# Joint image and text attention: x tile 3 loaded and transposed later, the last value chunk by key tile, one narrow value unit moved ahead of the shift strip

## The chip, the cores and the metric

The kernel runs on one core of one Trainium2 chip. The metric is device time in microseconds (us); the time before is the median of three runs, 116.81 us (116.59 to 117.2). The engines are named as in the profile: PE (TensorE, matrix products; PEld is its loading of the stationary operand), DVE (VectorE), ACT (ScalarE), POOL (GpSimd) and SP (SyncE, which here only issues loads and stores). Each engine takes its instructions in the order in which the program gives them to it, and waits for other engines through semaphores.

## The reference

Inputs are bf16: two batches of 256 image tokens and 32 text tokens, width D = 1152, a condition vector `c` for each batch, and for image and text each a modulation weight (D x 6D, of which the first three column blocks matter: shift, scale, gate), a query-key-value weight (D x 3D) and an output weight (D x D).

```python
mod = silu(c) @ wmod                       # shift, scale, gate
h   = layernorm(x) * (1 + scale) + shift   # image and text each
q, k, v = split(h @ wqkv)                  # image and text each
# tokens of text and image joined, one head of width D
p   = softmax(q @ k.T * D ** -0.5)
a   = p @ v
out = x + gate * (a @ wo)                  # image and text each
```

The change concerns the part up to the image values `v`.

## The kernel before

The 512 image tokens are four x tiles of 128 tokens (tiles 0 and 1 are batch 0, tiles 2 and 3 batch 1). The width D is nine key tiles of 128 rows (`KT`). The image values need the normalised x, transposed (so that width lies on the partitions) and multiplied by 1 + scale; the shift is left out of `hT_i` at first and comes in later, so that the value products can begin before the shift weights are there. The value product of a token tile is cut into three units of columns: two wide ones of 512 columns, written (tile, 0) and (tile, 1), and a narrow one of 128 columns (`v_rest`, line 339).

The weights come in four chunks of key tiles, `KC = [(0, 2), (2, 4), (4, 6), (6, 9)]`: of the scale weights the columns of these key tiles (`load_sc`), of the value weights their rows (`load_v`). All these loads stand in one queue, SP's, in the order of lines 103 to 114: x tiles 0 and 1, scale chunk 0, x tile 2, value chunk 0, x tile 3, then scale and value chunks in turn; the last value chunk comes in two pieces, key tile 6 and key tiles 7 and 8. Behind them come the shift weights (`w_sh_i`), the query weights and the rest.

The order of work is written out by hand (`manual_schedule`); there is no planner. For each x tile, DVE computes statistics in three pieces (`stats_of`, line 162), ACT takes the root (`std_of`, line 169), and DVE writes the normalised tile (`out_of`, lines 173 and 174). PE transposes it in nine steps (`x_transposes`, line 187): for tiles 1 to 3 the first eight go to one buffer of the pool `ps_mm` and the ninth to the single buffer of `ps_sm`. ACT empties them into `hT_i`: `evac_scaled` (line 192) multiplies by 1 + scale while it copies, one instruction for each key tile, `evac_low` (line 196) copies the other key tiles of the first buffer unscaled, in one instruction, and `evac_high` (line 199) the ninth. `mod_scale` (line 207) computes the scale factors of one chunk on PE and adds 1 on DVE (line 213); `apply_mod` (lines 223 to 232) then multiplies what was copied unscaled, on DVE, POOL or ACT by its last argument.

`v_part` (line 238) adds one chunk's key tiles to a wide unit. A unit holds its `ps_mm` buffer from its first chunk until its copy into `v_i` after the last (line 247; `evac`, lines 153 and 155, takes DVE and ACT in turn). `ps_mm` has seven buffers. Seven wide units are accumulated side by side (`SEVEN`): those of tiles 0 to 2, and (3, 0), which begins when tile 3's transposes have been copied out of theirs. The eighth, (3, 1), follows by itself (line 394).

Behind it comes the shift strip: `rows_for_cols` multiplies the shift weights as rows with the 32 columns of the condition (lines 367 and 371) and copies them on DVE; `select_cols` (lines 383 and 385) turns these rows into columns on PE, and `cols_out` writes them on DVE. Between strip and selection PE computes the narrow units of tiles 2 and 3, behind the selection those of tiles 0 and 1; then the shift is added to `hT_i` by three engines (lines 223, 226, 230), and the query products follow (line 444).

Of the kernel before, what the change touches and what calls it, by code (L numbers as in the profile page):

```python
# [14 lines left out]
def kernel(  # L15
# [14 lines left out]
    nc = tc.nc  # L30
# [4 lines left out]
    B, NI, D = x_img.shape  # L35
    NT = x_txt.shape[1]
    P = 128
    KT = D // P
    NTOK = NI + NT
    NIT = (B * NI) // P  # L40
    TPB = NI // P
    NTT = B * NT
    CH = 384
    NCH = D // CH
# [4 lines left out]
    KC = [(0, 2), (2, 4), (4, 6), (6, KT)]  # L49
    VW = 512  # L50
    NM = 1024
# [18 lines left out]
    def w_view(src):  # L70
        return src.rearrange("(kt p) n -> p kt n", p=P)
# [20 lines left out]
    def load_x(i):  # L92
        nc.sync.dma_start(x_i[:, i, :], xi_t[:, i, :])

    def load_sc(ch):
        k0, k1 = KC[ch]
        nc.sync.dma_start(w_sc_i[:, :, k0 * P:k1 * P], w_view(wmod_img)[:, :, D + k0 * P:D + k1 * P])

    def load_v(ch):
        k0, k1 = KC[ch]  # L100
        nc.sync.dma_start(w_v_i[:, k0:k1, :], w_view(wqkv_img)[:, k0:k1, 2 * D:3 * D])
# [3 lines left out]
    load_sc(0)  # L105
    load_x(2)
    load_v(0)
    load_x(3)
    for ch in range(1, len(KC)):
        load_sc(ch)  # L110
        if ch < len(KC) - 1:
            load_v(ch)
    for k0, k1 in ((6, 7), (7, KT)):
        nc.sync.dma_start(w_v_i[:, k0:k1, :], w_view(wqkv_img)[:, k0:k1, 2 * D:3 * D])
    K3 = ((0, 3), (3, 6), (6, KT))
# [35 lines left out]
    def evac(out_ap, in_ap):  # L151
        if evac_idx[0] % 2 == 0:
            nc.vector.tensor_copy(out_ap, in_ap)  # L153
        else:
            nc.scalar.copy(out_ap, in_ap)  # L155
        evac_idx[0] += 1

    def ln_stats(x_ap, np_, k0=0, k1=NCH, stats=None):
        if stats is None:
            stats = small.tile([P, NCH, 6], f32, tag="stats")  # L160
        for k in range(k0, k1):
            nc.vector.bn_stats(stats[0:np_, k, :], x_ap[:, k * CH:(k + 1) * CH])  # L162
        return stats

    def ln_std(stats, np_):
        mv = small.tile([P, 2], f32, tag="mv")
        nc.vector.bn_aggr(mv[0:np_, :], stats[0:np_, :, :])
        rstd = small.tile([P, 1], f32, tag="rstd")
        nc.scalar.activation(rstd[0:np_, :], mv[0:np_, 1:2], ACT.Sqrt, bias=eps_t[0:np_, :])
        return mv, rstd  # L170
# [10 lines left out]
    def x_transposes(i, n0=5):  # L181
        tps = (ps_mm.tile([P, n0, P], bf, tag="mm", name="tp"),
               ps_mm.tile([P, KT - n0, P], bf, tag="mm", name="tp") if n0 == 5 else
               ps_sm.tile([P, KT - n0, P], bf, tag="sm", name="tp"))
        for kt in range(KT):
            tp = tps[0][:, kt, :] if kt < n0 else tps[1][:, kt - n0, :]
            nc.tensor.transpose(tp, xn_i[:, i, kt * P:(kt + 1) * P], ident[:])  # L187
        return tps + (n0,)

    def evac_scaled(i, tps, n):  # L190
        for kt in range(n):
            nc.scalar.activation(hT_i[:, kt, i * P:(i + 1) * P], tps[0][:, kt, :], ACT.Identity,  # L192
                                 scale=mod_i[:, KT + kt, i // TPB:i // TPB + 1])

    def evac_low(i, tps, n):
        nc.scalar.copy(hT_i[:, n:tps[2], i * P:(i + 1) * P], tps[0][:, n:tps[2], :])

    def evac_high(i, tps):
        nc.scalar.copy(hT_i[:, tps[2]:KT, i * P:(i + 1) * P], tps[1][:])

    def mod_cols(wt, out_ps, j0, j1):
        for j in range(j0, j1):
            for kt in range(KT):
                nc.tensor.matmul(out_ps[:, j - j0, :], lhsT=wt[:, kt, j * P:(j + 1) * P], rhs=sT[:, kt, :],  # L204
                                 start=(kt == 0), stop=(kt == KT - 1))

    def mod_scale(ch, eng, own=True):
        k0, k1 = KC[ch]
        pool, tag = (ps_sm, "sm") if own else (ps_mm, "mm")
        mps = pool.tile([P, KT, B], f32, tag=tag)  # L210
        mod_cols(w_sc_i, mps, k0, k1)
        if eng == "dve":
            nc.vector.tensor_scalar_add(mod_i[:, KT + k0:KT + k1, :], mps[:, 0:k1 - k0, :], 1.0)  # L213
        else:
            nc.scalar.activation(mod_i[:, KT + k0:KT + k1, :], mps[:, 0:k1 - k0, :], ACT.Identity, bias=1.0)

    def apply_mod(kt, t0, t1, shift, eng):
        b = t0 // TPB
        sl = hT_i[:, kt, t0 * P:t1 * P]
        ap = mod_i[:, kt, b:b + 1] if shift else mod_i[:, KT + kt, b:b + 1]  # L220
        op = ALU.add if shift else ALU.mult
        if eng == 0:
            nc.vector.tensor_scalar(sl, sl, ap, None, op0=op)
        elif eng == 1:
            if shift:
                nc.gpsimd.tensor_scalar(sl, sl, 1.0, ap, op0=ALU.mult, op1=ALU.add)
            else:
                nc.gpsimd.tensor_scalar(sl, sl, ap, 0.0, op0=ALU.mult, op1=ALU.add)  # L228
        elif shift:
            nc.scalar.activation(sl, sl, ACT.Identity, bias=ap, scale=1.0)  # L230
        else:
            nc.scalar.activation(sl, sl, ACT.Identity, scale=ap)
# [2 lines left out]

    vacc = {}

    def v_part(i, half, ch):
        k0, k1 = KC[ch]
        if ch == 0:  # L240
            vacc[i, half] = ps_mm.tile([P, VW], f32, tag="mm", name=f"va{i}{half}")
        ps = vacc[i, half]
        for kt in range(k0, k1):
            nc.tensor.matmul(ps[:], lhsT=hT_i[:, kt, i * P:(i + 1) * P], rhs=w_v_i[:, kt, half * VW:(half + 1) * VW],  # L244
                             start=(kt == 0), stop=(kt == KT - 1))
        if k1 == KT:
            evac(v_i[:, i, half * VW:(half + 1) * VW], ps[:])


    def v_block(units, chs):  # L250
        for ch in chs:
            for (i, half) in units:
                v_part(i, half, ch)
# [6 lines left out]
    def stats_of(i, k0, k1):  # L260
        lns[i] = ln_stats(x_i[:, i, :], P, k0, k1, lns.get(i))

    def std_of(i):
        lns[i] = ln_std(lns[i], P)

    def out_of(i):
        ln_apply(x_i[:, i, :], P, xn_i[:, i, :], *lns[i])
# [19 lines left out]
    v_block([(0, 0), (0, 1), (1, 0), (1, 1)], [0])  # L287
    evac_low(1, tp1, 2)
    tps = x_transposes(2, KT - 1)
    stats_of(3, 0, NCH)  # L290
    evac_scaled(2, tps, 2)
    std_of(3)
    mod_scale(1, "dve", own=False)
    for n, kt in enumerate(range(*KC[1])):
        apply_mod(kt, 0, 2, False, n)
    evac_low(2, tps, 2)
    evac_high(2, tps)
    v_block([(2, 0), (2, 1)], [0])
    out_of(3)
    for kt in range(*KC[1]):  # L300
        apply_mod(kt, 2, 3, False, 0)
    v_block([(0, 0), (0, 1)], [1])
    tps = x_transposes(3, KT - 1)
    evac_high(3, tps)
    evac_scaled(3, tps, 4)
    evac_low(3, tps, 4)
    v_block([(1, 0), (1, 1)], [1])
    mod_scale(2, "dve")
    for kt in range(*KC[2]):
        apply_mod(kt, 0, 2, False, 0)  # L310
        apply_mod(kt, 2, 4, False, 1)
    v_block([(2, 0), (2, 1)], [1])
    v_block([(3, 0)], [0, 1])
    v_i = act.tile([P, NIT, D], bf, tag="A")
    SEVEN = [(i, half) for i in range(NIT) for half in range(2)][:7]
    for (i, half) in SEVEN[:5]:
        v_part(i, half, 2)
    mod_scale(3, "dve")
    for b in range(B):
        for n, kt in enumerate(range(*KC[3])):  # L320
            apply_mod(kt, b * TPB, (b + 1) * TPB, False, (n + b) % 3)
    for (i, half) in SEVEN[5:]:
        v_part(i, half, 2)
    for (i, half) in SEVEN:
        v_part(i, half, 3)

    for b in range(B):
        nc.gpsimd.tensor_copy(sTw[:, :, b, :], sT[:, :, b:b + 1].to_broadcast([P, KT, NT // 2]))  # L330
# [8 lines left out]
    def v_rest(i0, i1):  # L339
        ps = ps_mm.tile([P, TPB, P], f32, tag="mm")  # L340
        for kt in range(KT):
            for i in range(i0, i1):
                nc.tensor.matmul(ps[:, i - i0, :], lhsT=hT_i[:, kt, i * P:(i + 1) * P], rhs=w_v_i[:, kt, NM:D],  # L343
                                 start=(kt == 0 and i == i0), stop=(kt == KT - 1 and i == i1 - 1))
        return ps

    def v_rest_out(i0, i1, ps):
        evac(v_i[:, i0:i1, NM:D], ps[:])

    NGG = 4  # L350
    RC = 2 * P
# [23 lines left out]
    def rows_for_cols(wt, nm, lhs=None):  # L375
        gps = strip_rows(wt, sT32 if lhs is None else lhs)
        g_sb = work.tile([P, RC + P], bf, tag=nm, bufs=1, name=nm)
        evac(g_sb[:], gps[:])
        return g_sb
# [12 lines left out]
    ps = ps_mm.tile([P, VW], f32, tag="mm")  # L392
    for kt in range(KT):
        nc.tensor.matmul(ps[:], lhsT=hT_i[:, kt, 3 * P:4 * P], rhs=w_v_i[:, kt, VW:NM], start=(kt == 0), stop=(kt == KT - 1))  # L394
    evac(v_i[:, 3, VW:NM], ps[:])
    shr = rows_for_cols(w_sh_i, "shr")
    cps = ps_sm.tile([P, NCOL + B], f32, tag="sm")
    v_rest_out(TPB, NIT, v_rest(TPB, NIT))
    select_cols(shr, cps)
    cols_out(mod_i[:, 0:KT, :], cps, 0.0)  # L400
    vr = v_rest(0, TPB)
# [94 lines left out]
    for blk, wq in enumerate([w_q_t, w_k_t]):  # L496
        for j0 in range(0, KT, FG):
            jn = min(FG, KT - j0)
            ps = ps_mm.tile([P, FG, NTT], f32, tag="mm")
# [342 lines left out]
```

## Time and profile before

| | us |
|---|---|
| median of three runs | 116.81 (116.59 to 117.2) |
| the profiled execution | 116.89 |
| its span | 114.9 |
| PE busy | 108.6 (95%) |
| DVE, ACT, POOL busy | 53.4, 34.5, 28.0 |
| granted TensorE clock | 1.0 throughout |
| first matmul with a scale chunk | 8.03 |
| first wide value matmul | 10.23 |
| scale chunk 3's matmuls | 20.65 |
| shift strip | 28.76 |
| first query matmul | 32.11 |

The profile is of one execution. Its times count from the start of the span, and the measured time has some 2 us around the span. A line of the order of time has start, length, engine, line of the kernel, operation, the tiles written and read, and the count of instructions merged into it; in brackets stands how long the engine was idle before it and what ended that. Matmuls are pipelined: each wide one is given as 0.379 us though the next starts 0.216 us later, so the pace is read from start to start. A few records of matmuls are missing.

### The profile page before, as it was taken

To read this page: it belongs to the slowest core of one execution; us is meant where nothing else is said; L and a number is where in the kernel's file an instruction comes from. 1 tells how busy PE (TensorE), PEld (TensorE's weight loads), DVE (VectorE), ACT (ScalarE), POOL (GpSimd) and SP (SyncE) were. 2 spreads that over 40 slices of the span, in tenths; PEclk is the share of its full clock that TensorE was granted. 3 is DMA by queue.
4 is the path that set the end of the run, shared out by engine and by line. 5 is a ranking of instruction groups with operands and counts; after the bars stand their busy time and mean duration, and the time that the engine had idled before them with its cause. 6 is when DMAs were issued, how large, how long until landed. Compare 5 with 4: busy or idle time off the path is not lost.

```text
span 114.9 us, 2934 instructions
## 1 busy us (share of the span) xinstructions
PE 108.6 (95%) x1248; PEld 65.4 (57%) x1255; DVE 53.4 (47%) x137; ACT 34.5 (30%) x84; POOL 28.0 (24%) x59
## 2 busy tenths in 40 slices
PE   5948999999999999999999999999999999999990
PEld 1325564544954444477444545987788656667670
DVE  1687921354290212211742242136675813998571
ACT  2818960342380320121270221115565710001000
POOL 7000103460060000001315000000460460999100
DMA  3999999999999999999999999999999999962142
GB/s 87 276 362 361 371 384 377 411 412 411 411 404 405 412 416 402 412 412 411 405 408 412 396 411 410 406 410 405 411 408 407 407 411 397 388 244 106 37 157 69
DMA packets 22744, 40.89 MB, mean 356 GB/s; under 512 B 1279, under 2 KB 6539, under 8 KB 22731
## 3 DMA queue, kind: packets, MB, share of 16 engines
q1 hardware_dynamic: 21648, 39.64, 90.4%
q0 software_dynamic: 608, 0.88, 2.1%
q10 hardware_dynamic: 475, 0.18, 0.6%
q8 instruction: 10, 0.16, 0.5%
q14 instruction: 3, 0.02, 0.1%
HBM read 39.36 MB, written 1.34 MB: 354 GB/s over the span
## 4 chain that ended last, share of the span: by engine, by line
PE 90%; DMA 6%; SPq 1%; issue 1%; ACT 0%; DVE 0%
PE qkps L444 30%; PE ps L764 15%; PE va L244 12%; DMA w_sc_i<-in_wmod_img_dram 6%; PE aps L672 5%; PE ps L502 4%; PE sps L528 4%; PE gps L367 4%; PE mps L204 2%; PE ops L782 2%; PE ps L343 2%; PE tp L187 2%; PE ps L603 2%; PE ps L394 2%; PE gps L737 1%; PE sps L541 1%
## 5 line engine op out<-in xcount | busy, mean ns | idle before, releaser
L444 PE MATMUL qkps<-hT_i,t 128*128 128x512 bf16 x158 | 35.4, 379 | 0.2
L444 PEld LDWEIGHTS <-t 128*128 128x128 bf16 x162 | 15.6, 98 | 18.3
L764 PE MATMUL ps<-t,aT 128*128 128x384 bf16 x99 | 16.4, 326 | 0.0
L764 PEld LDWEIGHTS <-aT 128*128 128x128 bf16 x117 | 11.0, 98 | 6.9 <-issue 0.5
L244 PE MATMUL va<-w_v_i,hT_i 128*128 128x512 bf16 x60 | 14.1, 379 | 0.5 <-ACT hT_i L192 0.4
L748 POOL TENSOR_TENSOR w_og<-t,gb 128x384 bf16<-128x384 bf16 x9 | 8.8, 1016 | 4.1 <-issue 4.1
L244 PEld LDWEIGHTS <-hT_i 128*128 128x128 bf16 x63 | 5.8, 97 | 7.0 <-POOL hT_i L228 0.5
L770 DVE TENSOR_TENSOR tmp<-ps,gb 128x384 bf16<-128x384 f32 x11 | 6.1, 550 | 6.1 <-DMA gb<-mod_scratch 4.4
L428 DVE TENSOR_SCALAR qkT<-qkps 128x512 bf16<-128x512 f32 x4 | 2.8, 692 | 11.6 <-PE qkps L444 11.6
L162 DVE BATCH_NORM_STATS2 stats<-x_i 128x6 f32<-128x384 bf16 x12 | 5.8, 544 | 2.9 <-DMA x_i<-in_x_img_dram 2.9
L430 ACT ACTIVATE qkT<-qkps 128x512 bf16<-128x512 f32 x5 | 2.9, 596 | 13.5 <-PE qkps L444 13.5
L139 PE MATMUL wps<-wz 128*128 128x512 bf16 x16 | 5.6, 497 | 1.2 <-DVE wz L127 1.2
L228 POOL TENSOR_SCALAR hT_i<-hT_i,mod_img 128x256 bf16<-128x256 bf16 x5 | 2.5, 513 | 16.2 <-DVE mod_img L213 12.8
L153 DVE CAST qkT<-qkps 128x512 bf16<-128x512 f32 x4 | 2.8, 692 | 7.7 <-PE qkps L444 7.7
L155 ACT CAST qkT<-qkps 128x512 bf16<-128x512 f32 x5 | 2.8, 588 | 10.6 <-PE qkps L444 10.6
L522 POOL COPY px<-pb 128x64 bf16<-128x64 bf16 x4 | 1.0, 238 | 19.8 <-DVE pb L520 19.8
L771 DVE TENSOR_TENSOR o<-tmp,x_i 128x384 bf16<-128x384 bf16 x11 | 5.4, 486 | 0.4
L455 POOL TENSOR_SCALAR svn<-svr 128x128 bf16<-128x128 bf16 x1 | 0.3, 300 | 20.6 <-DVE svr L153 20.6
L685 DVE TENSOR_SCALAR aT<-aps,sv 128x288 bf16<-128x288 f32 (+2 forms) x11 | 4.3, 457 | 2.0 <-PE aps L672 2.0
L502 PEld LDWEIGHTS <-t 128*128 128x128 bf16 x162 | 4.9, 98 | 0.2
L502 PE MATMUL ps<-hT_t,t 128*128 128x64 bf16 x162 | 4.9, 193 | 0.0
L672 PE MATMUL aps<-pT,v_i 128*128 128x288 bf16 (+2 forms) x44 | 4.8, 264 | 0.0
(159 smaller groups left out, 143.7 us busy)
## 6 DMA issues: line engine op xcount, KB each, us to landing
t<-in_wmod_txt_dram SPq DMA_DIRECT2D x3, 2592.0 KB, 22.0
t<-in_wmod_img_dram SPq DMA_DIRECT2D x2, 2592.0 KB, 23.3
t<-in_wqkv_img_dram SPq DMA_DIRECT2D x6, 864.0 KB, 14.1
t<-in_wqkv_txt_dram SPq DMA_DIRECT2D x2, 2592.0 KB, 17.2
t<-in_wqkv_txt_dram SPq DMA_DIRECT2D x3, 864.0 KB, 14.5
t<-in_wo_img_dram SPq DMA_DIRECT2D x1, 2592.0 KB
t<-in_wo_txt_dram SPq DMA_DIRECT2D x3, 864.0 KB, 15.4
w_v_i<-in_wqkv_img_dram SPq DMA_DIRECT2D x4, 576.0 KB, 7.8
```

What stands on the lines that cost most here:

```text
L139: nc.tensor.matmul(ps[:], lhsT=wz[:, 0:P], rhs=wz[:], start=True, stop=True)
L162: nc.vector.bn_stats(stats[0:np_, k, :], x_ap[:, k * CH:(k + 1) * CH])
L244: nc.tensor.matmul(ps[:], lhsT=hT_i[:, kt, i * P:(i + 1) * P], rhs=w_v_i[:, kt, half * VW:(half + 1) * VW], start=(kt == 0), stop=(kt == K ...
L367: nc.tensor.matmul(gps[32 * g:32 * g + 32, 0:RC], lhsT=lhs[:, kt, :], rhs=wt[:, kt, g * RC:(g + 1) * RC], start=(kt == 0), stop=(kt == KT ...
L444: nc.tensor.matmul(pss[j - j0][:], lhsT=wq[:, kt, j * P:(j + 1) * P], rhs=hT_i[:, kt, :], start=(kt == 0), stop=(kt == KT - 1))
L502: nc.tensor.matmul(ps[:, j - j0, :], lhsT=wq[:, kt, j * P:(j + 1) * P], rhs=hT_t[:, kt, :], start=(kt == 0), stop=(kt == KT - 1))
L528: nc.tensor.matmul(sps[:], lhsT=qkT[:, ft, b, q0:q0 + P], rhs=qkT[:, KT + ft, b, :], start=(ft == 0), stop=(ft == KT - 1))
L672: nc.tensor.matmul(bank[:, off:off + c1 - c0], lhsT=lhsT, rhs=rhs, start=(first[id(bank)] == n), stop=(final[id(bank)] == n))
L748: nc.gpsimd.tensor_mul(w_og[:, dt, 0:CH], w_o_i[:, dt, NG0:D], gb[:, B - 1, NG0:D])
L764: nc.tensor.matmul(ps[:, 0:cw], lhsT=aT[:, dt, t0:t0 + P], rhs=rhs, start=(dt == DTS[0]), stop=(dt == DTS[-1]))
L770: nc.vector.tensor_mul(tmp[:, 0:cw], ps[:, 0:cw], gb[:, b, cs])
L771: nc.vector.tensor_add(o[:, cs], tmp[:, 0:cw], x_i[:, i, cs])
```

## The change

Four things are moved; the set of matmuls and loads stays the same.

- x tile 3 is loaded behind value chunk 1 instead of behind value chunk 0.
- Its statistics, root and normalisation move on DVE and ACT behind the multiplications of chunk 1; its transposes move on PE behind all chunk-1 matmuls and the scale factors of chunk 2. Six of its key tiles, not four, are now scaled while they are copied, so chunk 2's later multiplications cover only tiles 0 to 2. The matmuls of (3, 0) for chunks 0 and 1 move behind the five units' chunk 2.
- The last chunk runs over its key tiles in two passes, key tile 6 for all seven units, then key tiles 7 and 8; before, each unit took its three key tiles at once.
- The narrow unit of tile 2 moves ahead of the shift strip, with a copy of its own on DVE; only that of tile 3 stays between strip and selection.

```diff
     load_v(0)
-    load_x(3)
     for ch in range(1, len(KC)):
         load_sc(ch)
         if ch < len(KC) - 1:
             load_v(ch)
+        if ch == 1:
+            load_x(3)
...
-    def v_part(i, half, ch):
-        k0, k1 = KC[ch]
+    def v_part(i, half, ch, kts=None):
+        k0, k1 = kts or KC[ch]
...
     tps = x_transposes(2, KT - 1)
-    stats_of(3, 0, NCH)
     evac_scaled(2, tps, 2)
-    std_of(3)
     mod_scale(1, "dve", own=False)
     for n, kt in enumerate(range(*KC[1])):
         apply_mod(kt, 0, 2, False, n)
     evac_low(2, tps, 2)
     evac_high(2, tps)
     v_block([(2, 0), (2, 1)], [0])
-    out_of(3)
     for kt in range(*KC[1]):
         apply_mod(kt, 2, 3, False, 0)
-    v_block([(0, 0), (0, 1)], [1])
-    tps = x_transposes(3, KT - 1)
-    evac_high(3, tps)
-    evac_scaled(3, tps, 4)
-    evac_low(3, tps, 4)
-    v_block([(1, 0), (1, 1)], [1])
+    stats_of(3, 0, NCH)
+    std_of(3)
+    out_of(3)
+    v_block([(0, 0), (0, 1), (1, 0), (1, 1), (2, 0), (2, 1)], [1])
     mod_scale(2, "dve")
     for kt in range(*KC[2]):
         apply_mod(kt, 0, 2, False, 0)
-        apply_mod(kt, 2, 4, False, 1)
-    v_block([(2, 0), (2, 1)], [1])
-    v_block([(3, 0)], [0, 1])
+        apply_mod(kt, 2, 3, False, 1)
+    tps = x_transposes(3, KT - 1)
+    evac_high(3, tps)
+    evac_scaled(3, tps, 6)
+    evac_low(3, tps, 6)
     v_i = act.tile([P, NIT, D], bf, tag="A")
     SEVEN = [(i, half) for i in range(NIT) for half in range(2)][:7]
     for (i, half) in SEVEN[:5]:
         v_part(i, half, 2)
+    v_block([(3, 0)], [0, 1])
     mod_scale(3, "dve")
...
     for (i, half) in SEVEN[5:]:
         v_part(i, half, 2)
-    for (i, half) in SEVEN:
-        v_part(i, half, 3)
+    k0, k1 = KC[3]
+    for kts in ((k0, k0 + 1), (k0 + 1, k1)):
+        for (i, half) in SEVEN:
+            v_part(i, half, 3, kts)
...
     def v_rest_out(i0, i1, ps):
-        evac(v_i[:, i0:i1, NM:D], ps[:])
+        evac(v_i[:, i0:i1, NM:D], ps[:, 0:i1 - i0, :])
...
     evac(v_i[:, 3, VW:NM], ps[:])
+    vr = v_rest(TPB, TPB + 1)
+    nc.vector.tensor_copy(v_i[:, TPB:TPB + 1, NM:D], vr[:, 0:1, :])
     shr = rows_for_cols(w_sh_i, "shr")
     cps = ps_sm.tile([P, NCOL + B], f32, tag="sm")
-    v_rest_out(TPB, NIT, v_rest(TPB, NIT))
+    v_rest_out(TPB + 1, NIT, v_rest(TPB + 1, NIT))
     select_cols(shr, cps)
```

## The prediction

> **What bounds the kernel now.** I read the chain that ended last first, because it says which engine a gain must come from; then the order of time between 10 and 33 us, which is where the change lies; then the landing times of single loads, by asking for the DMA issues of one short stretch each.
>
> ```profile
> PE 90%; DMA 6%; SPq 1%; issue 1%; ACT 0%; DVE 0%
> ```
>
> From 8.0 us to 112.1 us the chain is TensorE (PE). The 6% DMA are the wait for the first scale chunk, which the change doesn't touch. So the change can win only where PE stands still, and loses where it makes PE stand still. The order of time shows how little it stands still in the stretch concerned (start, length, engine, line, what, count):
>
> ```profile
> 10.23 1.89 PE L244 MATMUL va<-w_v_i,hT_i 128*128 128x512 bf16 x7 [0.36 <-ACT hT_i L192]
> 11.58 1.48 DVE L162 BATCH_NORM_STATS2 stats<-x_i 128x6 f32<-128x384 bf16 x3
> 11.95 0.67 PE L187 MATMUL tp<-ident,xn_i 128*128 128x128 bf16 x9
> 12.61 0.52 PEld L204 LDWEIGHTS <-w_sc_i 128*128 128x128 bf16 x18 [0.17 <-DMA w_sc_i<-in_wmod_img_dram]
> 13.26 0.16 DVE L213 TENSOR_SCALAR mod_img<-mps 128x4 f32<-128x4 f32 x1
> 13.56 0.78 ACT L196 COPY hT_i<-tp 128x768 bf16<-128x768 bf16 x1
> 13.62 0.55 POOL L228 TENSOR_SCALAR hT_i<-hT_i,mod_img 128x256 bf16<-128x256 bf16 x1 [9.56 <-DVE mod_img L213]
> 13.93 0.58 DVE L174 TENSOR_SCALAR xn_i<-x_i,mv,rstd 128x1152 bf16<-128x1152 bf16 x1
> 14.22 0.40 PEld L244 LDWEIGHTS <-hT_i 128*128 128x128 bf16 x3 [0.25 <-POOL hT_i L228]
> 14.95 0.67 PE L187 MATMUL tp<-ident,xn_i 128*128 128x128 bf16 x9
> 15.65 0.27 ACT L199 COPY hT_i<-tp 128x128 bf16<-128x128 bf16 x1 [1.14 <-PE tp L187]
> 15.81 1.15 ACT L192 ACTIVATE hT_i<-tp,mod_img 128x128 bf16<-128x128 bf16 x4
> 16.77 4.04 PE L244 MATMUL va<-w_v_i,hT_i 128*128 128x512 bf16 x18
> 16.83 0.61 ACT L196 COPY hT_i<-tp 128x512 bf16<-128x512 bf16 x1
> 20.65 0.82 PE L204 MATMUL mps<-sT,w_sc_i 128*128 128x2 bf16 x27
> ```
>
> Matmul durations overlap, so I count start to start. 18 wide matmuls from 16.77 to 20.65 are 215.6 ns each; the first eight (10.23 to 11.95) have the same pace. Nine transposes are 0.50, and 18 scale matmuls 0.46 (16.31 to 16.77). Idle PE between 10.23 and 26.72 is then only 0.16 (tile 2's transposes are issued by 12.45, scale chunk 1 comes at 12.6) and 0.14 (second key tile of (0,0), chunk 1: possible at 14.16, started at 14.30 behind POOL). Sum 0.30: this is all that the order of the stretch can give back.
>
> Loads land as follows (issue plus time to landing): value chunk 0 10.23, scale chunk 1 12.53, value chunk 1 14.03, scale chunk 2 15.71, value chunk 2 17.13. An x tile takes 0.77 (from scale chunk 0 at 7.95 to x tile 2 at 8.72).
>
> The strip, further on (the third line is the copy that its selection waits for):
>
> ```profile
> 28.76 1.17 PE L367 MATMUL gps<-t,sT 128*32 128x256 bf16 x36
> 30.01 1.18 PE L343 MATMUL ps<-w_v_i,hT_i 128*128 128x128 bf16 x18
> 30.12 0.56 DVE L153 CAST shr<-gps 128x384 bf16<-128x384 f32 x1 [2.51 <-PE gps L371]
> 31.03 0.19 PE L383 MATMUL cps<-sel,shr 128*128 128x8 bf16 x2
> ```
>
> **The change part by part.** No matmul is added or removed: transposes, wide and narrow units are the same in number. Only waits differ.
>
> *Loads.* With x tile 3 behind value chunk 1, scale chunk 1 lands at 12.53 - 0.77 = 11.76, value chunk 1 at 13.26, x tile 3 at 14.03; everything behind it is unchanged, as the bytes ahead are the same. On SP's queue the issue of x tile 3 (0.47) moves behind two others, and scale chunk 2 is issued at 7.91 as before. PE starts scale chunk 1 at 12.45, and the DVE factor comes at 13.10. Tile 2's second scaled copy on ACT still ends at 13.23 (so its matmul starts at 13.28 against 13.30), and POOL's multiplication, 0.36 after the factor's start and 0.55 long, ends at 14.01: the second key tile starts at 14.14 against 14.30. Gain 0.16. Ends: 0 (ACT keeps the old start) and 0.30 (all idle time). I take 0.16, the row of POOL.
>
> *Transposes of tile 3 behind scale chunk 2.* Tile 2's four chunk-0 matmuls run from 13.03 to 13.92 (the second at 13.28), then from (0,0)'s first chunk-1 matmul twelve matmuls (2.59) and 18 scale ones (0.46) bring PE to the transposes at 16.97. DVE has to be through out_of(3). ACT's low copy of tile 2 no longer stands behind the root of tile 3: it starts at 13.10, 0.78 long; DVE's two small multiplications start at 13.96 (0.08 behind it, as at 14.42 now) and take 0.32 to the next start, so the statistics begin at 14.28. x tile 3 (14.03) is in time by 0.25. For tile 2 the statistics begin at 8.77 and the normalised tile is there at 11.67: 2.90. So 14.28 + 2.90 = 17.18, plus 0.12 to the first transpose: 17.30. PE waits 17.30 - 16.97 = +0.33. Behind the waiting transposes stand all 14 wide matmuls up to scale chunk 3; behind out_of(3) on DVE stands the factor of chunk 2, ready at 17.15 to 17.31, and its two multiplications (to 17.85), covered by the transposes; uncovered they would cost 0.5. Ends: 0 (statistics from 13.95), and +1.81 if x tile 3 landed only with scale chunk 2 at 15.71 (nearest later landing; statistics 1.48 later).
>
> *The accumulator of (3,0).* ps_mm has seven buffers; six hold the units of tiles 0 to 2, the seventh tile 3's transposes. (3,0) can start only when ACT has emptied that one. Now: first transpose 14.95, ACT's high copy 15.65 (0.70 later), four scaled copies 0.265 apart from 15.81, the low copy from 16.83 to 17.44; (3,0) starts at 17.63, by which time it is free. After: six scaled copies in the same pattern put the low copy 1.71 behind the high one, and 256 columns take 0.37 (the 128x256 copy at 31.23): the end is 0.70 + 1.71 + 0.37 = 2.78 behind the first transpose. PE gets to (3,0) after 0.50 + 10 x 0.2156 = 2.66. With 0.07 for the release it waits 2.85 - 2.66 = +0.19. Ends: 0, if ACT is a little quicker, and +0.9, if the six copies don't overlap (0.368 each). The row of before alone shows no wait at (3,0); carried over as it stands it would make the sum +0.44, 117.3. The Trainium skill ("Perfetto Trace Analysis", Matmuls) asks that independent groups of matmuls rotate through different banks, so that the emptying of one lies beside the next group; by that rule a unit that must take the bank just being emptied waits, which is the +0.63. No row of before shows such a wait.
>
> *Last chunk by key tile.* The seven units then end 0.43 apart rather than 0.65; two engines copy at 0.69 and 0.59, so two fit into 0.86 and all keep pace; the next accumulator comes from the unit that ended 2.6 us before. Cost 0; uncovered, one copy of 0.69. Below nothing: the 0.25 weight-load wait for POOL at 22.39 goes, but the matmuls lost only some 0.04 there.
>
> *One narrow unit ahead of the strip.* Nine narrow matmuls (18 in 1.02: 0.51) go in front; their own DVE copy (about 0.27) is covered by the strip's 1.25, else it costs that. But the cover between strip and selection shrinks from 1.02 to 0.51. The strip's copy starts 0.11 behind the strip's end and takes 0.56, and a dependent matmul starts some 0.11 behind it (weight load 0.05, matmul 0.06): 0.78. PE waits 0.78 - 0.51 = +0.27. Behind it stand the shift columns and their additions, at the same distance as now. Ends: 0, and 0.40 if the copy took the 0.69 of a wide one.
>
> Sum: -0.16 + 0.33 + 0.19 + 0.27 = **+0.63 us**. The profiled execution took 116.89 (span 114.9 and 1.99 around it), 0.08 above the median of 116.81; so 117.5, 0.6% over that median. About 0.5% (0.58 us) is what a measurement of this kernel can tell from no change, so this stands just outside.
>
> **The rivals.** B, not slower: tile 3's DVE work is through before PE arrives. Place: out_of(3); it decides if the statistics begin by 13.95. For it: x tile 3 is there at 14.03 by the spacing and DVE has little else; against it: the small multiplications wait for ACT until 13.96. Then -0.16 + 0.19 + 0.27 = +0.30: 117.2.
>
> C, x tile 3 is late: behind the two 576 KB chunks it lands up to scale chunk 2's 15.71. Against it: the landings follow the order of issue in all rows above. +0.63 + 1.48: 119.0.
>
> D, faster: the loads are served side by side, so that other neighbours also bring value chunk 0, before which PE stood 0.38 (9.85 to 10.23), and no new wait appears: -0.30 to -0.68, 116.6 to 116.2. For it: that chunk took 1.51 at its place against 1.42 later; against it: what lies ahead of it is unchanged.
>
> **How the numbers follow.** Forecast 0.55, B 0.24, C 0.12, D 0.09. Slower than 117.39: 0.38 of the forecast's 0.55 (its own spread is 117.1 to 118.0), C and 0.02 of B: 0.52. Faster than 116.23: 0.04 of D. Within: 0.44. The range 116.8 to 118.3 leaves out C and half of D.
>
> **What would show it.** Scale chunk 1's matmuls at about 12.45; tile 3's statistics at 14.3; its first transpose at 17.3 with a wait for L174's DVE line; the first chunk-0 matmul of (3,0) waiting for ACT's low copy; scale chunk 3 at 21.0 against 20.65; the selection waiting for the strip's copy. If the statistics wait for a DMA, C is right; if PE shows no gap before tile 3's transposes, B. A prediction gone wrong would be a wait at a place not named, above all between 21 and 28 us.

## The result and the profile after

The changed kernel takes 117.23 us (median of 22 runs, 116.81 to 117.75) against 116.71 us (22 runs) for the kernel before: a ratio of 1.0041 (taken over all runs, not from the two medians), 95% interval 1.0023 to 1.0058, or +0.48 us (+0.27 to +0.68). The profiled execution took 117.53, its span is 115.5. The chain that ended last is now, by engine:

```profile
PE 82%; DMA 9%; SPq 5%; issue 1%; DVE 0%
```

The DMA share has grown from 6% to 9%, and it is another load: no longer the first scale chunk, but value chunk 2. The 5% SPq are SP's issuing of the loads, up to that of value chunk 2. The order of time of the changed kernel (columns as before; line numbers differ by one from those before):

```profile
9.34 1.89 PE L245 MATMUL va<-w_v_i,hT_i 128*128 128x512 bf16 x7 [0.24 <-DMA w_v_i<-in_wqkv_img_dram]
11.71 0.59 PE L205 MATMUL mps<-sT,w_sc_i 128*128 128x2 bf16 x18
13.62 1.48 DVE L163 BATCH_NORM_STATS2 stats<-x_i 128x6 f32<-128x384 bf16 x3
15.87 0.59 PE L205 MATMUL mps<-sT,w_sc_i 128*128 128x2 bf16 x18
15.93 0.58 DVE L175 TENSOR_SCALAR xn_i<-x_i,mv,rstd 128x1152 bf16<-128x1152 bf16 x1
16.50 0.16 DVE L214 TENSOR_SCALAR mod_img<-mps 128x4 f32<-128x4 f32 x1
16.56 0.51 PEld L188 LDWEIGHTS <-xn_i 128*128 128x128 bf16 x9 [0.19 <-DVE xn_i L175]
```

```profile
18.00 3.18 PE L245 MATMUL va<-w_v_i,hT_i 128*128 128x512 bf16 x13 [0.76 <-DMA w_v_i<-in_wqkv_img_dram]
18.94 0.42 ACT L197 COPY hT_i<-tp 128x256 bf16<-128x256 bf16 x1
21.02 0.82 PE L205 MATMUL mps<-sT,w_sc_i 128*128 128x2 bf16 x27
...
30.99 0.56 DVE L154 CAST shr<-gps 128x384 bf16<-128x384 f32 x1 [0.96 <-PE gps L370]
31.60 0.27 ACT L156 CAST v_i<-ps 128x128 bf16<-128x128 f32 x1 [1.78 <-PE ps L342]
31.60 0.11 PEld L382 LDWEIGHTS <-shr 128*128 128x128 bf16 x2 [0.21 <-DVE shr L154]
```

In this execution the first loads came early, and the first wide matmul runs at 9.34 instead of 10.23. Scale chunk 1 (11.71) no longer waits for its load. Then the wait at tile 3's transposes (behind DVE L175) and the wait of the selection (0.21, behind the strip's copy) stand where the prediction put them. But between them stands one that it did not have: the first chunk-2 matmul waits 0.76 for value chunk 2. That load was issued at 7.47 and took, by the list of issues for this stretch (x1, KB, us to landing),

```profile
w_v_i<-in_wqkv_img_dram SPq DMA_DIRECT2D x1, 576.0 KB, 10.5
```

so it landed at 17.97, 3.1 behind scale chunk 2 (14.87); before it took 8.7 and landed 1.42 behind scale chunk 2. The predicted wait of (3, 0) for ACT is not there in this execution, because PE comes to (3, 0) only when its buffer has long been copied out. All the early start is lost at the load: scale chunk 3 begins at 21.02 against 20.65, and the first query matmul at 32.70 against 32.11. From there to the end of the span both kernels take the same 82.8.

Because the arrival of the first loads varies from execution to execution, the experiments are compared by stretches: from the first wide matmul to scale chunk 3 (before: 10.42) and from there to the first query matmul (before: 11.46). The first of these is not quite free of the arrival: where the first loads come early, tile 2's transposes wait for DVE's normalisation, and from the first wide matmul to scale chunk 2 it takes 6.53 (first profile) and 6.57 (experiment 4) instead of the 6.30 of experiments 1, 7, 9 and 12.

### The profile page after: what moved, and what is told of

Read it like the earlier page. It is cut to its first block, busy times and chain, and to the rows that moved or that the text cites. A ratio compares the mean times of both kernels' runs of the same rounds, so it can differ in the third digit from the quotient of the medians.

```text
span 115.5 us, 2940 instructions
## 1 busy us (share of the span) xinstructions
PE 109.7 (95%) x1248; PEld 65.8 (57%) x1255; DVE 54.0 (47%) x138; ACT 34.6 (30%) x86; POOL 27.7 (24%) x59
## 4 chain that ended last, share of the span: by engine, by line
PE 82%; DMA 9%; SPq 5%; issue 1%; DVE 0%
PE qkps L445 30%; PE ps L765 15%; DMA w_v_i<-in_wqkv_img_dram 9%; PE va L245 7%; PE aps L673 5%; PE ps L503 4%; PE sps L529 4%; PE gps L366 4%; SPq L101 2%; SPq L93 2%; PE ops L783 2%; PE ps L342 2%; PE ps L393 2%; PE ps L604 2%; SPq L97 1%; PE gps L738 1%
## 5 line engine op out<-in xcount | busy, mean ns | idle before, releaser
L765 PE MATMUL ps<-t,aT 128*128 128x384 bf16 x99 | 16.4, 326 | 0.0
L229 POOL TENSOR_SCALAR hT_i<-hT_i,mod_img 128x256 bf16<-128x256 bf16 (+1 forms) x5 | 2.3, 469 | 16.8 <-ACT hT_i L193 8.6
```

The costliest lines, as they stand in the source:

```text
L765: nc.tensor.matmul(ps[:, 0:cw], lhsT=aT[:, dt, t0:t0 + P], rhs=rhs, start=(dt == DTS[0]), stop=(dt == DTS[-1]))
```

## The experiments

Two theories. 1, the recorded one: tile 3's DVE chain, the accumulator of (3, 0) and the selection cost the time. 2: value chunk 2 lands late in many executions, the changed order needs it earlier, and its landing sets the time whatever stands before it.

| kernel | ratio (95% interval) | first wide matmul | value chunk 2 landed | to scale chunk 3 | on to the queries |
|---|---|---|---|---|---|
| before | 1 | 10.23 | 17.13 | 10.42 | 11.46 |
| changed | 1.0041 (1.0023 to 1.0058) | 9.34 | 17.97 | 11.68 | 11.68 |
| changed, again | (one time) | 9.83 | 17.94 | 11.14 | 11.68 |
| 1 changed, old narrow units | 1.0038 (1.0018 to 1.0059) | 10.16 | 17.14 | 10.71 | 11.47 |
| 2 before, new narrow units | 1.0024 (1.0006 to 1.0043) | 9.88 | 16.78 | 10.37 | 11.68 |
| 3 changed, no statistics | 1.0054 (1.0034 to 1.0074) | 9.60 | 17.88 | 11.29 | 11.68 |
| 4 changed, old load order | 1.0043 (1.0020 to 1.0065) | 9.51 | 16.47 | 10.98 | 11.68 |
| 5 changed, chunk 1's rows | 1.0025 (1.0009 to 1.0041) | 9.72 | 17.88 | 10.70 | 11.67 |
| 6 changed, all waits out | 1.0011 (0.9999 to 1.0024) | 9.87 | 16.83 | 10.61 | 11.46 |
| 7 changed, tiny matmuls | 1.0061 (1.0043 to 1.0078) | 10.00 | 17.01 | 10.70 | 11.68 |
| 8 x tile 3 behind scale chunk 1 | 1.0036 (1.0021 to 1.0051) | 9.91 | 16.88 | 10.71 | 11.47 |
| 9 changed, four copies | 1.0033 (1.0018 to 1.0048) | 9.83 | 16.75 | 10.60 | 11.68 |
| 10 before, last chunk by key tile | 0.9997 (0.9981 to 1.0014) | 10.02 | 16.91 | 10.37 | 11.46 |
| 11 before, new load order | 1.0262 (1.0202 to 1.0322) | 9.90 | 16.80 | 14.38 | 11.46 |

A landing is the issue plus the time to landing, which the list rounds to 0.1, so it is good to about 0.05.

**1. The narrow units put back.**

```diff
-    vr = v_rest(TPB, TPB + 1)
-    nc.vector.tensor_copy(v_i[:, TPB:TPB + 1, NM:D], vr[:, 0:1, :])
...
-    v_rest_out(TPB + 1, NIT, v_rest(TPB + 1, NIT))
+    v_rest_out(TPB, NIT, v_rest(TPB, NIT))
```

> The changed kernel with the narrow units of tiles 2 and 3 both back between strip and selection. Both theories agree that the selection waits for the strip's copy by 0.2 to 0.27 us in the changed kernel and not here. Expected: 0.2 to 0.27 us less than the changed kernel, so about +0.25 us (ratio 1.002) against the kernel before instead of +0.48, and no weight-load wait of the selection for the strip's copy. If the ratio stays at 1.004, the selection's wait was covered by something later.

The stretch behind scale chunk 3 falls from 11.68 to 11.47, the value of before. The ratio (1.0038) doesn't show it: its interval holds the expected 1.002 as well as the change's 1.0041. In this execution value chunk 2 came in time, and the lines show theory 1's other waits alone:

```profile
16.52 0.58 DVE L175 TENSOR_SCALAR xn_i<-x_i,mv,rstd 128x1152 bf16<-128x1152 bf16 x1
17.15 0.51 PEld L188 LDWEIGHTS <-xn_i 128*128 128x128 bf16 x9 [0.19 <-DVE xn_i L175]
17.67 3.37 PE L245 MATMUL va<-w_v_i,hT_i 128*128 128x512 bf16 x13
19.55 0.42 ACT L197 COPY hT_i<-tp 128x256 bf16<-128x256 bf16 x1
20.02 0.53 PEld L245 LDWEIGHTS <-hT_i 128*128 128x128 bf16 x3 [0.22 <-issue]
```

Scale chunk 2 began at 16.46, so PE could have transposed at 16.92 and did at 17.16: a wait of 0.24. The weights of (3, 0) come at 20.02, right behind the end of ACT's low copy at 19.97.

**2. The narrow units alone.**

```diff
+    vr = v_rest(TPB, TPB + 1)
+    nc.vector.tensor_copy(v_i[:, TPB:TPB + 1, NM:D], vr[:, 0:1, :])
...
-    v_rest_out(TPB, NIT, v_rest(TPB, NIT))
+    v_rest_out(TPB + 1, NIT, v_rest(TPB + 1, NIT))
```

> The kernel before with the narrow unit of tile 2 alone moved ahead of the strip. Expected if the terms of the sum add: +0.2 to +0.27 us (ratio 1.0017 to 1.0023), with the selection's weight load waiting some 0.2 us for the strip's copy. If the shift weights were what the strip waited for, the moved unit would fill that wait and the ratio would be 1.000 or below.

Ratio 1.0024, and the last stretch is 11.68 here too. The selection waits for the strip's copy:

```profile
30.84 0.11 PEld L383 LDWEIGHTS <-shr 128*128 128x128 bf16 x2 [0.21 <-DVE shr L153]
```

Its wait is worth 0.21 to 0.22 us, on its own and in the changed kernel; nothing covers it. That the strip waited for its weights is out.

**3. No statistics for tile 3.**

```diff
-    stats_of(3, 0, NCH)
-    std_of(3)
-    out_of(3)
+    nc.vector.tensor_scalar(xn_i[:, 3, :], x_i[:, 3, :], lns[2][0][:, 0:1], lns[2][1][:, :], op0=ALU.subtract, op1=ALU.mult)
```

> The changed kernel with tile 3 normalised by tile 2's mean and root: its statistics, root and reciprocal are left out (so tile 3's part of the result is another one), which takes 2.3 us out of the DVE chain ahead of tile 3's transposes. Theory 1 (the recorded one: DVE's chain for tile 3 sets the transposes): the transposes wait no more, -0.2 to -0.33 us against the changed kernel, ratio about 1.002. Theory 2 (value chunk 2's landing sets the five units behind the transposes, so PE only waits in another place): the gap moves from the transposes to the first chunk-2 matmul, and the time stays at the changed kernel's, ratio 1.003 to 1.005.

The transposes follow scale chunk 2's matmuls without a gap (15.96, 16.41), and then PE waits 0.81 for value chunk 2:

```profile
16.41 0.66 PE L188 MATMUL tp<-ident,xn_i 128*128 128x128 bf16 x9
17.88 3.18 PE L245 MATMUL va<-w_v_i,hT_i 128*128 128x512 bf16 x13 [0.81 <-DMA w_v_i<-in_wqkv_img_dram]
```

The ratio is not lower (1.0054). In such an execution the DVE chain costs nothing: theory 2.

**4. The old load order under the new order of work.**

```diff
     load_v(0)
+    load_x(3)
     for ch in range(1, len(KC)):
...
-        if ch == 1:
-            load_x(3)
```

> The changed kernel with x tile 3 loaded where it was, behind value chunk 0; the order of work is the changed one. Theory 1: statistics still start at about 14.3 behind the small multiplications, scale chunk 1 comes 0.77 us later, which costs the 0.16 gained; ratio 1.005 to 1.006. Theory 2: value chunk 2 lands at the same place in the queue, so its wait is unchanged and the time stays at 1.003 to 1.005; PE's wait for scale chunk 1 only shortens the later one.

1.0043: no different from the change, but the interval also holds theory 1's 1.005 to 1.006, so the ratio can't tell the 0.16 us. The waits at the transposes (16.54 to 16.77) and from the first chunk-2 matmul on (17.29 to 20.49, 3.20 for 14 matmuls worth 3.02) are the same. Scale chunk 1 (landed at 11.9) came just as PE was through tile 2's transposes, which were late themselves (the 6.57 above, which is also why this stretch is 10.98 and not 10.70), so in this execution the place of the load cost nothing; what it costs otherwise is not shown. It also says nothing on value chunk 2, which came in time in this execution.

**5. Chunk 2 on chunk 1's rows.**

```diff
-            nc.tensor.matmul(ps[:], lhsT=hT_i[:, kt, i * P:(i + 1) * P], rhs=w_v_i[:, kt, half * VW:(half + 1) * VW],
+            nc.tensor.matmul(ps[:], lhsT=hT_i[:, kt, i * P:(i + 1) * P], rhs=w_v_i[:, kt - 2 if ch == 2 else kt, half * VW:(half + 1) * VW],
```

> The changed kernel whose chunk-2 value matmuls read chunk 1's weight rows (so the values are others); the load of value chunk 2 stays, but nothing waits for it before the eighth wide unit. Theory 1 (recorded: tile 3's DVE chain, the accumulator of (3, 0) and the selection cost the time): unchanged against the changed kernel, ratio 1.003 to 1.005. Theory 2 (in many executions value chunk 2 lands only at about 17.9 and PE waits for it 0.75 to 0.8 us): the five units start right behind tile 3's transposes, (3, 0) waits some 0.2 us for ACT instead, and the time falls by up to 0.74 us in those executions, ratio 0.998 to 1.001.

In the profile value chunk 2 landed late (17.88) and nobody waited for it: the stretch to scale chunk 3 is 10.70 instead of 11.14 to 11.68, and from scale chunk 2 on it is 4.40 instead of 4.84 and 5.15 in the two profiles of the changed kernel. So the late landing costs 0.44 to 0.75 us in those executions. The ratio is 1.0025, between the two expectations, and its interval overlaps the change's, so it doesn't show by how much late landings raise the median; but as it stays above 1 they are not the whole cost.

**6. All waits taken out.**

```diff
+    nc.vector.tensor_scalar(xn_i[:, 3, :], x_i[:, 3, :], lns[2][0][:, 0:1], lns[2][1][:, :], op0=ALU.subtract, op1=ALU.mult)
...
-    evac_scaled(3, tps, 6)
-    evac_low(3, tps, 6)
+    evac_scaled(3, tps, 4)
+    evac_low(3, tps, 4)
+    for kt in range(*KC[2]):
+        apply_mod(kt, 3, 4, False, 1)
```

(with the edits of 1, 3 and 5)

> The changed kernel with every wait named so far taken out: tile 3 normalised by tile 2's mean and root (its statistics left out), chunk-2 value matmuls on chunk 1's rows (so the values are others), four scaled copies instead of six (chunk 2's multiplication of tile 3 on POOL), and both narrow units between strip and selection. If these waits are all that the change costs, only the earlier scale chunk 1 is left: -0.16 us, ratio 0.998 to 1.000. If it stays above 1.002, a cost has not been named.

The ratio, 1.0011 (0.9999 to 1.0024), lies between the two expectations, but the stretch to scale chunk 3 is 0.19 longer than before instead of 0.16 shorter. A cost was left, and the lines name it:

```profile
16.63 0.66 PE L188 MATMUL tp<-ident,xn_i 128*128 128x128 bf16 x9
16.81 0.16 DVE L214 TENSOR_SCALAR mod_img<-mps 128x4 f32<-128x4 f32 x1 [2.31 <-PE mps L205]
17.00 0.60 DVE L224 TENSOR_SCALAR hT_i<-hT_i,mod_img 128x256 bf16<-128x256 bf16 x2
17.34 0.10 PEld L245 LDWEIGHTS <-hT_i 128*128 128x128 bf16 x1 [0.23 <-DVE hT_i L224]
17.35 3.30 PE L245 MATMUL va<-w_v_i,hT_i 128*128 128x512 bf16 x14
17.66 2.49 PEld L245 LDWEIGHTS <-hT_i 128*128 128x128 bf16 x13 [0.22 <-DVE hT_i L224]
```

The first chunk-2 matmul could run at 17.13, behind the nine transposes, and runs at 17.35: the path from scale chunk 2's matmuls through the factor and DVE's multiplication takes 1.18 (16.17 to 17.35), and transposes and scale matmuls cover only 0.96 of it. The second multiplication costs another 0.11 (3.13 for the 14 matmuls). So -0.14 + 0.22 + 0.11 = +0.19. Before, eight wide matmuls stood between scale chunk 2 and its first use.

**7. Twelve tiny matmuls more.**

```diff
     warm(11)
+    tiny = ps_mm.tile([P, VW], f32, tag="mm", name="tiny")
+    for _ in range(12):
+        nc.tensor.matmul(tiny[:, 0:2], lhsT=wz[:, 0:P], rhs=wz[:, 0:2], start=True, stop=True)
```

> The changed kernel with twelve tiny matmuls of two columns (and their weight loads) on PE behind the warm-up, where PE waits for the first scale chunk anyway. The trace shows one packet of the instruction queue, 0.96 us of one DMA engine, starting between 15.6 and 16.2 us in every kernel so far. If it is PE's own instructions, it comes 24 PE instructions earlier, by 1.0 to 2.6 us, and value chunk 2 is no more held up by it (landing about 1.4 us behind scale chunk 2, ratio 1.002 to 1.004); another load may be held up instead. If it is another engine's, it stays at 15.6 to 16.2 and nothing changes (1.004).

The instruction packet starts at 15.63, no earlier than in experiment 3 (15.64); the other profiles have it at 15.9 to 16.4, not at 16.2 at most as the expectation says. Counted from the first wide matmul it comes 5.6 behind, against 6.1 and 6.6 in the two profiles of the changed kernel: a shift of 0.4 to 1.0, short of the 1.0 to 2.6 or at its edge. The next two packets do move that far, to 28.69 and 40.41 from 31.7 to 32.3 and 42.5 to 43.4 in the other profiles of the changed order. So those two hang on the count of PE's instructions, and for the first that is not shown. Value chunk 2 lands at 17.01, but it is punctual in 6 and 8 too, where the packet comes at the same time as in the late ones (15.9 to 16.0). The ratio (1.0061) is higher than the change's, with overlapping intervals, though the stretches (10.70 and 11.68) are shorter. In the profile 0.2 us are lost far behind the change: from the first query matmul to the end it takes 82.96, where the others take 82.7 to 82.8, and the loss lies at one matmul of the attention product (line 676); its cause stays open. Up to the queries the profile is the change's with all loads in time, and its waits are theory 1's:

```profile
16.93 0.16 DVE L214 TENSOR_SCALAR mod_img<-mps 128x4 f32<-128x4 f32 x1
16.99 0.50 PEld L188 LDWEIGHTS <-xn_i 128*128 128x128 bf16 x9 [0.18 <-DVE xn_i L175]
17.13 0.60 DVE L224 TENSOR_SCALAR hT_i<-hT_i,mod_img 128x256 bf16<-128x256 bf16 x2
17.79 1.84 PEld L245 LDWEIGHTS <-hT_i 128*128 128x128 bf16 x10 [0.22 <-DVE hT_i L224]
19.37 0.42 ACT L197 COPY hT_i<-tp 128x256 bf16<-128x256 bf16 x1
19.84 0.53 PEld L245 LDWEIGHTS <-hT_i 128*128 128x128 bf16 x3 [0.21 <-issue]
```

**8. x tile 3 behind scale chunk 1, with the other fixes.**

```diff
         load_sc(ch)
+        if ch == 1:
+            load_x(3)
...
+    stats_of(3, 0, 1)
     evac_scaled(2, tps, 2)
...
+    stats_of(3, 1, NCH)
     for kt in range(*KC[1]):
         apply_mod(kt, 2, 3, False, 0)
-    stats_of(3, 0, NCH)
```

(with the edits of 1 and the four copies of 6)

> A version put together from the findings: x tile 3 loaded behind scale chunk 1 and ahead of value chunk 1, its statistics begun in the idle time of DVE ahead of chunk 1's factors, four scaled copies, both narrow units between strip and selection; transposes where the change puts them. Theory 1: no wait at the transposes, none for the accumulator, none at the selection, so -0.16 us, ratio 0.9985. Theory 2: value chunk 2 is needed even earlier (about 17.4), so that in executions with a late landing 0.4 to 0.5 us are lost; ratio 1.000 to 1.003.

1.0036, where theory 1 had 0.9985 and theory 2 at most 1.003. There is no wait at the transposes, but the factor's path costs the same 0.22 + 0.11 as in 6 (scale chunk 2 at 16.32, first chunk-2 matmul at 17.49), and the 16 matmuls ahead of it take 3.62 instead of the 3.50 of the change, for a reason that stays open. It doesn't beat the kernel before.

**9. Four scaled copies.** The diff is the second part of 6's.

> The changed kernel with four scaled copies of tile 3 instead of six (chunk 2's multiplication of tile 3 on POOL instead), which empties the accumulator's buffer earlier by 0.29 us. Recorded theory (the accumulator of (3, 0) waits 0.18 to 0.19 us for ACT's low copy): -0.18 us against the changed kernel, ratio 1.002 to 1.003, and 3.02 us instead of 3.20 from the first chunk-2 matmul to scale chunk 3. Rival: where value chunk 2 lands late, PE waits for it and the buffer is free by then, so nothing is gained: ratio 1.004.

The 14 matmuls from the first chunk-2 one on take 3.10 (17.33 to 20.43) instead of 3.20:

```profile
17.33 3.27 PE L245 MATMUL va<-w_v_i,hT_i 128*128 128x512 bf16 x14
20.43 0.82 PE L205 MATMUL mps<-sT,w_sc_i 128*128 128x2 bf16 x27
```

So the accumulator of (3, 0) waits 0.10; the other 0.08 are DVE's second multiplication. The ratio, 1.0033, is lower, but not beyond the intervals.

**10. The last chunk by key tile alone.**

```diff
-    for (i, half) in SEVEN:
-        v_part(i, half, 3)
+    k0, k1 = KC[3]
+    for kts in ((k0, k0 + 1), (k0 + 1, k1)):
+        for (i, half) in SEVEN:
+            v_part(i, half, 3, kts)
```

> The kernel before with the last chunk by key tile alone (two passes over the seven units). Recorded: costs nothing, since the copies keep pace and no key tile was waited for; ratio 0.999 to 1.001. Rival: the units end later and closer together, the copies on DVE and ACT then hold up the strip's buffer or its copy by up to 0.69 us: ratio up to 1.006.

0.9997: it costs nothing and brings nothing.

**11. The load order alone.**

```diff
     load_v(0)
-    load_x(3)
     for ch in range(1, len(KC)):
...
             load_v(ch)
+        if ch == 1:
+            load_x(3)
```

> The kernel before with x tile 3 loaded behind value chunk 1, and the order of work left as it was. DVE has tile 3's statistics ahead of chunk 1's factors, so that it waits for x tile 3 (landing at about 14.0 instead of under 11.6) and the factors come at about 15.8 instead of 13.26: PE waits some 2.4 us at (0,0)'s second chunk; part of it can't be made good anywhere, ratio 1.015 to 1.022. If the loads were not taken in the order of the queue, x tile 3 would be there earlier and the ratio stays under 1.005.

x tile 3 lands at 13.67, as the order of the queue has it, and DVE waits for it ahead of chunk 1's factor:

```profile
13.70 1.48 DVE L163 BATCH_NORM_STATS2 stats<-x_i 128x6 f32<-128x384 bf16 x3 [2.40 <-DMA x_i<-in_x_img_dram]
15.37 0.10 DVE L214 TENSOR_SCALAR mod_img<-mps 128x4 f32<-128x4 f32 x1
15.53 2.21 PE L245 MATMUL va<-w_v_i,hT_i 128*128 128x512 bf16 x6 [2.19 <-DVE mod_img L214]
```

The ratio, 1.0262, is above the 1.015 to 1.022 expected: the clock fell as well (last section). Three of the four executions, the profiled one among them, have a mean granted clock of 0.986 and take 120.23 to 120.6; the fourth kept 0.999 and takes 118.54, which is 1.017 times the kernel before (116.58) and inside the expectation. So the load can't be moved back alone: the work has to move with it.

**12. The changed kernel again.**

> The changed kernel once more, for a second profile. If value chunk 2 lands in time (under 17.2): a wait of 0.23 us at tile 3's transposes, 0.18 at (3, 0) and 0.21 at the selection, and 22.35 to 22.4 us from the first wide matmul to the first query matmul, against 21.88 before. If it lands at 17.9 again: no wait at (3, 0), a wait for the load instead.

Value chunk 2 lands late once more, 2.6 behind scale chunk 2:

```profile
16.13 0.59 PE L205 MATMUL mps<-sT,w_sc_i 128*128 128x2 bf16 x18
16.82 0.51 PEld L188 LDWEIGHTS <-xn_i 128*128 128x128 bf16 x9 [0.19 <-DVE xn_i L175]
17.95 3.18 PE L245 MATMUL va<-w_v_i,hT_i 128*128 128x512 bf16 x14 [0.45 <-DMA w_v_i<-in_wqkv_img_dram]
20.97 0.82 PE L205 MATMUL mps<-sT,w_sc_i 128*128 128x2 bf16 x27
```

The first chunk-2 matmul is at 17.95 here and at 18.00 in the first profile, though the first wide matmul came 0.49 later: in these executions the load sets the time and hides the wait in front of it. Both took more (117.46 and 117.53) than the median of 117.23, so other executions probably had the load in time; how often was not measured.

## Why the prediction was right or wrong

The direction, the place within the range and the size stand: +0.63 forecast, +0.48 measured (+0.27 to +0.68). The likelier side of the chances did not come: 0.52 stood on more than 117.39, and 117.23 is under it. The rivals are out as they were priced: x tile 3 was never late for the changed order (C), no gain appeared (D), and PE did wait at tile 3's transposes (B). A slip in the chances: the range leaves out all of D's 116.2 to 116.6, not half. Point by point, by the profiles in which all loads came in time (1, 7 and 9):

- *Loads, -0.16.* Right: -0.14, by profiles of two kernels; the old load order under the new order of work (4) doesn't show it. In 7, the way from the first wide matmul to the first of tile 2 is 2.80 instead of 2.85, and the dense block loses 0.05 instead of 0.14 behind POOL.
- *Transposes, +0.33.* The mechanism is right (DVE's normalisation, named by the weight loads), the size was 0.23. PE arrives where it was expected (6.76 behind the first wide matmul; forecast 6.74); the first transpose follows the normalised tile by 0.05, where 0.12 had been put, and the chain runs 2.89 as forecast. The step "its two multiplications (to 17.85), covered by the transposes" failed: with the wait gone, they are not covered (0.22 and 0.11 in 6), so taking away the DVE chain's 0.23 alone would bring almost nothing. That also makes rival B's price wrong: the factor of chunk 2 is late next.
- *Accumulator of (3, 0), +0.19.* The mechanism is right, the size 0.10 (3.20 against 3.10 in 9). The forecast let PE arrive without the 0.08 that it loses to chunk 2's second multiplication, a term that it put at nothing.
- *Last chunk, 0.* Right (10).
- *Narrow unit, +0.27.* 0.21 to 0.22 (2, and 1 by its removal): the selection follows the copy by 0.06, where 0.11 had been put.

The sum of these is -0.14 + 0.23 + 0.08 + 0.10 + 0.21 = +0.48; the two stretches in 7 show +0.28 + 0.22 = +0.50. That this equals the measured +0.48 is partly chance, because both profiles of the changed kernel itself went another way. The step that failed there is "everything behind it is unchanged, as the bytes ahead are the same": value chunk 2 landed at 17.94 and 17.97 instead of 17.13, though it landed at about 17 in 1, 6, 7 and 9 with the same order of loads. The forecast gave its landing and not its need. Before, PE needs it at 18.50 (four chunk-1 and four (3, 0) matmuls follow 16.77), which leaves 1.4; in the changed order it is needed right behind the transposes, at about 17.3 to 17.8, which leaves almost nothing. So a load that is late by 0.8 would cost nothing before (there it was never late in a profile) and sets the time after. Why it is late in some kernels and executions (changed kernel twice, 3 and 5) and punctual in the others stays open: neither the time of the first loads nor the start of the instruction packet separates them. The last section shows what the late ones have in common.

## What to carry to other kernels

When work is put in front of other work, ask of every operand of what is now first: when does it land or come out of its chain, and how much slack did it have. The changed order put two things, a load and a scale factor, directly ahead of their use, where eight matmuls of cover had stood before; each wait hid the next, so that removing one gained little. And a reserve between two dependent steps (1.02 us behind the strip) is no waste until the copy it covers has been measured: in the changed kernel it takes 0.72 from the strip's end to the selection.

## What the runs showed of the hardware

In experiment 11 a single gap of 2.19 us on PE was followed by a low granted clock. Columns of the stretches: from and to, length, busy time of PE, PEld, DVE, ACT and POOL with counts, granted clock, DMA share, GB/s:

```profile
12.90:15.50 2.60, 0.44 (x2) 0.11 (x2) 1.73 (x5) 0.02 (x1) 0.00 (x0) 1.00 1.09 382
15.50:16.50 1.00, 0.97 (x4) 0.32 (x4) 0.88 (x3) 1.00 (x3) 0.54 (x1) 0.88 1.10 379
16.50:17.00 0.50, 0.50 (x2) 0.15 (x1) 0.42 (x3) 0.13 (x1) 0.00 (x0) 0.50 1.04 352
18.50:19.50 1.00, 1.00 (x5) 0.44 (x4) 0.00 (x0) 0.77 (x4) 0.00 (x0) 0.50 1.05 407
20.00:21.00 1.00, 1.00 (x22) 0.69 (x21) 0.39 (x3) 0.52 (x2) 0.09 (x1) 1.00 1.05 417
```

From about 16.3 to 19.7 PE had half its clock: the four wide matmuls at 18.48 took 1.47 to the next scale matmul instead of 0.86, and the transposes 0.96 instead of 0.50. The Trainium skill ("TensorE: Matmul & The Clock Gate", "Why this matters for your kernels") advises against idle gaps of more than about 3 us; here 2.2 us, with a PE busy before and after, were enough in the profiled execution, and two more of the four have the same mean clock; the fourth kept its clock, but it has no trace that would show its gap. The 0.76 of the changed kernel and the 1.54 ahead of the first scale chunk before left the clock at 1.00.

The profile also shows ten packets of the instruction queue in each execution, and the one at about 16 us holds one DMA engine for 0.96 us. The Trainium skill ("Runtime: NRT & Kernel Launch", "Instruction fetch mechanics") says that instructions are fetched in blocks of 16 KiB, 256 instructions, and that the cost of crossing a block is mostly hidden; the size agrees (0.16 MB for ten), and in experiment 7 the 24 added instructions of PE bring the second and third packet forward by 2.1 to 3.6 us.

The records of single packets bring the late landing and this packet together. Every load counts sixteen shares. In all fourteen profiles fifteen shares of value chunk 2 have landed by 16.16 to 16.81; the last one lands at 16.45 to 17.14 in the ten punctual profiles, and at 17.83 to 17.96 in the four late ones. Less the packet's 0.96 that would be 16.87 to 17.00, as punctual as the others. In the first profile and in experiment 5 the record that completes the last share starts within 0.02 us of the end of the instruction packet (16.9 in both). This fits an instruction packet that goes ahead of the last share on the same DMA engine. It is not shown: the records don't name the engine, no run moved this packet away, and why it would meet the last share in some executions only is open.
